# The last quarter of the first expert's output weights, narrowed in tiles 1 and 2 of the first expert instead of during attention

## The chip, the cores and the metric

The kernel runs on one core of a Trainium2 chip. The metric is the device time of one execution in microseconds (us). Engines are called as in the profile: PE (matmuls; PEld its weight loads), DVE, ACT, POOL and SP; each works through its own queue in the order in which the program issues to it. SP issues most of the DMAs here, POOL and ACT issue some.

## The reference

```python
# attention: 4 batches, 12 heads, 448 x 448 scores, head size 64
scores = einsum('bhij,hg->bgij', scale * q @ k.T, w_pre)      # heads mixed
attn   = einsum('bgij,gh->bhij', softmax(scores), w_post)     # mixed again
x      = (attn @ v)  as 1792 tokens x 768
# first expert (d_ff = 1024)
h = x @ w_in;  solu = h * softmax(h);  ln = layernorm(solu) * g_ln
x = ln @ w_out
# second expert (d_ff = 2048)
out = relu(x @ w_in2)**2 @ w_out2
```

## The kernel before

The four weight matrices of the experts arrive as 64-bit floats, which no engine computes with. The kernel turns them into 32-bit floats itself ("narrowing"): it takes pieces of 128 rows by 256 columns, loads the raw 64-bit words, squares the high word on ACT (to see which numbers are too small), makes a mask of that on POOL, puts the sign, exponent and mantissa together with three integer operations on DVE, and stores the 32-bit piece to a DRAM buffer (w1iD, w1oD, w2iD, w2oD), from which the matmul stages load it later. Every matrix is then split in two parts, a high part (a copy rounded by ACT) and a low part (the difference, on POOL), and each product takes three matmuls.

Four stages follow one another: attention (90 slots, to 382 us of the span), the first expert (14 tiles of 128 tokens, numbered m = 0 to 13), a short join, and the second expert (16 rounds).

**Narrowing in attention.** `w1pieces` (lines 413 and 414) lists 24 pieces of the first expert's input weights and 24 of its output weights (8 row blocks of 3 pieces). A planner in the slot loop gives the loads an even share of slots 5 to 70. For each piece POOL issues a load of 256 KB (`load_w1`, line 419), ACT squares, DVE does three operations of 256 columns, POOL two (`flush`, lines 102 and 103), ACT multiplies a piece of output weights by the layer norm's g (`scale_w1`, line 440), and SP stores 128 KB.

**Narrowing in the first expert.** `w2stream` (line 844) is a generator for the second expert's pieces. Its first step issues four loads on SP; the next two each issue a square on ACT and a mask on POOL; then every piece takes three steps, one DVE operation each (A, B, C: lines 887, 891, 893). Step A also issues the square and the mask of the piece after the next; step B the store of the piece before. `steps2(n)` takes n steps, and `rate(m, n)` says how many at each of four places of tile m: 0 up to tile 3 (`GT` is 3), n in tiles 4 to 12, n // 2 in tile 13.

**A tile of the first expert**, in the order of issue:

1. the load of tile m + 2's activations (SP, `load_x`);
2. `h1(m)`: 36 matmuls of 512 columns into one of two accumulators, which alternate;
3. `norm1(m)` up to its first pause: row maximum (DVE line 773), exponential (ACT 776), product with h (DVE 779), statistics (DVE 782, 784), root (POOL 786, 787);
4. place 1 for steps, then `nb` (DVE 790);
5. `zt(m - 1)`: eight transposes on PE (809), copied by ACT (811), low part by DVE (812);
6. in tiles 0 to 3 the rest of `norm1(m)` (ACT 794), then place 2 for steps;
7. `split_x(m + 2)`: high part by ACT (762), low part by POOL (763, 768 columns);
8. loads and splits of two row blocks of w_out, kk = 2m and 2m + 1 (SP 743, ACT 748, POOL 749), in tiles 0 to 3;
9. places 3 and 4 for steps, with an `out1` at each from tile 4 on: 24 matmuls that need the transposes of three tiles and all eight split blocks of w_out.

So the first `out1` comes in tile 4, and PE's own order in between is h1(2), transposes of tile 1, h1(3), transposes of tile 2, h1(4), transposes of tile 3, out1.

Of the kernel before, what the change touches and what calls it, by code (L numbers as in the profile page):

```python
# [11 lines left out]
AF = mybir.ActivationFunctionType  # L12
# [6 lines left out]
def kernel(  # L19
# [16 lines left out]
    nc = tc.nc  # L36
# [3 lines left out]
    NT, DM = out.shape  # L40
    F1 = w1_in.shape[1]
# [13 lines left out]
    scale = 1.0 / float(D) ** 0.5  # L55
# [7 lines left out]
    w1oD = dram.tile([F1, DM], F32, name="w1oD")  # L63
# [11 lines left out]
    g_sb = const.tile([128, F1 // 128], F32, name="g_sb")  # L75
# [64 lines left out]
    for b in range(B):  # L140
        for (i0, n) in CHUNKS:
# [10 lines left out]
            elif odd:  # L152
                k = nks[0] - 1
                order = [(1, k)] + order[:-2] + [(0, k)]
            for h, k in order:
                r = len(range(k, (n0, n - n0)[h], nks[h]))
# [9 lines left out]
    kk = {}  # L166
# [241 lines left out]
    WP = 256  # L408
# [2 lines left out]
    w1s = {}  # L411
    w1t = {}
    w1pieces = [(w1_in, w1iD, k, o) for k in range(CC) for o in range(0, F1, WP)]
    w1pieces += [(w1_out, w1oD, k, o) for k in range(F1 // 128) for o in range(0, DM, WP)]

    def load_w1(i):
        src, dst, k, o = w1pieces[i]
# [75 lines left out]
    def h1(m):  # L493
        t = xs.pop(m)
        pool = psi_p if m % 2 else psh_p
        ps = pool.tile([128, 2, 512], F32, tag="h", name="ps_h")
        for cc in range(CC):
            for (a, w) in ((0, 0), (0, 1), (1, 0)):
                for u in range(2):
                    nc.tensor.matmul(  # L500
                        out=ps[:, u],
                        lhsT=t[:, a, cc],
                        rhs=w1i[cc][:, w, u * 512:(u + 1) * 512],
                        start=(cc == 0 and a == 0 and w == 0),
                        stop=(cc == CC - 1 and a == 1),
                    )
            yield True
        hps[m] = ps

    def run(part):  # L510
        for _ in part:
            pass
# [215 lines left out]
    K1 = F1 // 128  # L728
# [12 lines left out]
    def load_w1_out(kk):  # L741
        r = wi1_p.tile([128, DM], F32, tag="wraw", name="w1oraw", bufs=3)
        nc.sync.dma_start(out=r, in_=w1oD[kk * 128:(kk + 1) * 128, :])
        return r

    def split_w1_out(kk, r):
        t = m1_p.tile([128, 2, DM], F32R, name=f"w1o{kk}")
        nc.scalar.copy(t[:, 0], r)
        nc.gpsimd.tensor_tensor(out=t[:, 1], in0=r, in1=t[:, 0].bitcast(F32), op=ALU.subtract)
        w1o.append(t)  # L750

    def load_x(m):
        r = wi1_p.tile([128, CC * 128], F32, tag="wraw", name="xraw", bufs=3)
        r = r.rearrange("p (c t) -> p c t", c=CC)
        nc.sync.dma_start(
            out=r, in_=xD[:, m * 128:(m + 1) * 128].rearrange("(c p) t -> p c t", p=128)
        )
        return r

    def split_x(m, r):  # L760
        t = m1b_p.tile([128, 2, CC, 128], F32R, tag="xs", name="xs", bufs=2)
        nc.scalar.copy(t[:, 0], r)
        nc.gpsimd.tensor_tensor(out=t[:, 1], in0=r, in1=t[:, 0].bitcast(F32), op=ALU.subtract)  # L763
        xs[m] = t
# [32 lines left out]
    GT = 3  # L797
# [37 lines left out]
    NE = F2 // FE  # L835
    KE = FE // 128
    FIRST = 60
    w2pieces = []
    for e in range(NE):
        w2pieces += [(w2_in, w2iD, c, e * FE) for c in range(CC)]  # L840
        w2pieces += [(w2_out, w2oD, e * KE + f, o) for f in range(KE) for o in range(0, DM, WP)]
    narrowed = []

    def w2stream(todo, nr, home):

        raws, ts, ready = {}, {}, []

        def load(i):
            if i in todo:
                src, dst, k, o = w2pieces[i]  # L850
                raws[i] = home(i, True)
                nc.sync.dma_start(out=raws[i], in_=src[k * 128:(k + 1) * 128, o:o + WP])

        def words(i):
            pair = raws[i].bitcast(U32).rearrange("p (n two) -> p n two", two=2)
            return pair[:, :, 0], pair[:, :, 1]

        def mask(i):

            if i in todo:  # L860
                t = ts[i] = home(i, False)
                nc.scalar.activation(out=t, in_=words(i)[1].bitcast(F32), func=AF.Square)  # L862
                nc.gpsimd.tensor_scalar(  # L863
                    out=t, in0=t, scalar1=2.0**-30, scalar2=2.0 - 2.0**-23, op0=ALU.is_ge, op1=ALU.mult
                )

        def store():
            i = ready.pop(0)
            src, dst, k, o = w2pieces[i]
            nc.sync.dma_start(out=dst[k * 128:(k + 1) * 128, o:o + WP], in_=ts.pop(i))  # L870
            narrowed.append(i)

        a = todo[0]
        for i in range(nr - 1):
            load(a + i)
        yield True
        mask(a)
        yield True
        mask(a + 1)
        yield True  # L880
        for i in todo:
            load(i + nr - 1)
            mask(i + 2)
            low, high = words(i)
            bits = ts[i].bitcast(U32)
            stt = nc.vector.scalar_tensor_tensor
            stt(out=bits, in0=high, scalar=3, in1=bits, op0=ALU.logical_shift_left, op1=ALU.bitwise_and)
            yield True
            if ready:
                store()  # L890
            stt(out=bits, in0=high, scalar=0xC0000000, in1=bits, op0=ALU.bitwise_and, op1=ALU.bitwise_or)
            yield True
            stt(out=bits, in0=low, scalar=29, in1=bits, op0=ALU.logical_shift_right, op1=ALU.bitwise_or)
            raws.pop(i)
            ready.append(i)
            yield True
        store()
        yield True
# [3 lines left out]
            return m1b_p.tile([128, WP], I64, tag="nraw", name="nraw", bufs=5)  # L902
        return m1b_p.tile([128, WP], F32, tag="nt", name="nt", bufs=5)

    stream = w2stream(range(FIRST), 5, home1)

    NTILE = NT // 128

    def rate(m, n):
        return 0 if m <= GT else n if m < NTILE - 1 else n // 2  # L910

    def steps2(n):
        for _ in range(n):
            next(stream, None)
# [4 lines left out]
    for m in range(NTILE):  # L919
        if m + 2 < NTILE:  # L920
            xr[m + 2] = load_x(m + 2)
        if m:
            run(h1(m))
        norm = norm1(m)
        next(norm)
        steps2(rate(m, 4))
        next(norm)
        if m > 0:
            zt(m - 1)
        if m <= GT:  # L930
            run(norm)
        steps2(rate(m, 6))
        if m + 2 < NTILE:
            split_x(m + 2, xr.pop(m + 2))
        for kk in range(len(w1o), min(K1, len(w1o) + 2)):
            wr[kk] = load_w1_out(kk)
        for kk in sorted(wr):
            split_w1_out(kk, wr.pop(kk))
        if m > GT and (m - 1) % GT == 0:
            outs += [((m - 1) // GT - 1, cc) for cc in range(CC)]  # L940
        for i in range(2):
            if outs:
                out1(*outs.pop(0))
            if i == 0:
                run(norm)
            steps2(rate(m, 4))


    outs += [((NTILE - 1) // GT, cc) for cc in range(CC)]
# [228 lines left out]
    def lows():  # L1178
        while low:
            r, f, t = low.pop(0)  # L1180
            hi, lo = [gt[:, a, f, t * HT:(t + 1) * HT] for a in range(2)]
            nc.vector.tensor_tensor(out=lo, in0=r, in1=hi.bitcast(F32), op=ALU.subtract)  # L1182
# [138 lines left out]
        t = wi2a_p.tile([128, HT], F32, tag=f"xb{i // 2 % 2}{i % 2}", name="nt", bufs=2)  # L1321
        return t[:, 0:WP]

    stream = w2stream(range(FIRST, len(w2pieces)), 4, home2)
    parts = []
    for q in range(NQ):
        p = q // NE
        work = plan(q)
        if q == NE - 1:
            parts = [((1, name), c) for name in ORDER for c in range(HC)]  # L1330
            load_xc(*parts[0][0])
            load_xc(*parts[HC][0])
        seq = SEQ_P if q < SW else SEQ
        for k, x in enumerate(seq):
            if isinstance(x, str):
                prod(q, x)
                after(q, x)
            elif q:
                y2(q - 1, x)
            lows()  # L1340
            for f, a in work.pop(k, []):
                f(*a)
            if parts:
                t, c = parts[0]
                if q == NE - 1 and (t[1] in ("p2", "p4") or t[1] in ("p7", "p3") and k < 7):
                    t = None
                if t:
                    parts.pop(0)
                    split_xc(*t, c)
                    i = ORDER.index(t[1]) + 2  # L1350
                    if c == HC - 1 and i < len(ORDER):
                        load_xc(1, ORDER[i])
            if q <= NE - 3:
                if q or k > 5:
                    steps2(2)
                if q == NE - 3 and k == len(seq) - 1:
                    run(stream)
                    next(mx)
            elif q == NE - 2 and k:
                next(mx, None)  # L1360
        assert not work
        if q < NE:
            assert len(narrowed) >= min(12 * (q + 2) + 6, len(w2pieces)), (q, len(narrowed))
    assert not parts
    for x in YO:
        y2(NQ - 1, x)
# [60 lines left out]
```

## Time and profile before

| what | value |
|---|---|
| median of three runs | 1085.63 us (1083.68 to 1088.42) |
| the profiled execution | 1085.38 us, of which its span (first to last instruction) 1083.6 us |
| PE busy | 1035.0 us, 96% of the span |
| DVE, ACT, POOL busy | 63%, 52%, 62% |
| mean granted clock of PE | 0.992 |

The span is the time from the first to the last instruction; 1.8 us of the execution lie outside it. Busy shares are averages over stages. What a change in one stage is worth has to be read in that stage, from the gaps of PE and from what ends them.

### The profile page before, as it was taken

How to read it: one execution, taken by the hardware profiler on the slowest of the kernel's cores; microseconds unless marked ns; L12 is line 12 of the kernel's file. 1: busy time of each engine (PE TensorE's matmuls, PEld its weight loads, DVE VectorE, ACT ScalarE, POOL GpSimd, SP SyncE). 2: the span in 40 equal slices, each digit the busy share in tenths (PEclk: the TensorE clock that was granted, in tenths of full speed). 3: DMA queues.
4: the chain of work that ended last, by engine and by line, in shares of the span. 5: the costliest groups of instructions: out<-in, count | busy, mean ns of one | idle time of the engine just before them, and what ended most of it. 6: DMA issues, size and time to landing. Idle time of an engine off the chain costs nothing.

```text
span 1083.6 us, 30106 instructions
## 1 busy us (share of the span) xinstructions
PE 1035.0 (96%) x12220; PEld 889.7 (82%) x12220; DVE 679.4 (63%) x1131; ACT 562.5 (52%) x1195; POOL 675.1 (62%) x868
## 2 busy tenths in 40 slices
PE   7798989989899899999999999999999999999998
PEld 3565656666666788999999989999999999999998
DVE  3576868767786346888876445787656833444444
ACT  4567667768777445444443446444334554444432
POOL 4567878878875737565645256666535757666620
PEclk9999999999999999999999999999999999999999
DMA  7678887878876624656555545444545521111102
GB/s 245 178 216 253 221 243 240 253 225 260 247 210 199 185 69 150 204 162 203 167 169 165 199 162 164 148 142 141 188 157 196 200 94 59 59 59 59 59 30 102
DMA packets 115914, 181.06 MB, mean 167 GB/s; under 512 B 24224, under 2 KB 87200, under 8 KB 115776
## 3 DMA queue, kind: packets, MB, share of 16 engines
q1 hardware_dynamic: 100276, 127.79, 38.5%
q0 software_dynamic: 12608, 48.55, 14.8%
q10 hardware_dynamic: 2892, 2.80, 0.9%
q8 instruction: 96, 1.57, 0.6%
q14 instruction: 42, 0.34, 0.1%
HBM read 102.42 MB, written 38.14 MB: 130 GB/s over the span
## 4 chain that ended last, share of the span: by engine, by line
PE 52%; POOL 3%; DVE 3%; issue 3%; DMA 2%; ACT 1%; SPq 0%; POOLq 0%; ACTq 0%
PE ps_y L1240 20%; PE ps_h L1169 17%; PE ps_o L823 8%; PE ps_h L500 7%; POOL ti L1097 1%; DMA w2oD<-nt 1%; DVE st L782 1%; DVE e L779 1%; POOL to L1105 1%; PE ps_tr L809 1%; DMA nraw<-in_moe_w_out_dram 0%; DMA ra<-w2iD 0%; ACT e L776 0%; POOL s L1077 0%; DVE nm L773 0%
## 5 line engine op out<-in xcount | busy, mean ns | idle before, releaser
L1240 PE MATMUL ps_y<-to,gt 128*128 128x384 f32 x1332 | 241.8, 336 | 2.5 <-POOL to L1105 1.8
L1240 PEld LDWEIGHTS ps_y<-to,gt 128*128 128x128 f32 x1332 | 233.6, 188 | 4.8 <-POOL to L1105 2.1
L1169 PE MATMUL ps_h<-xc,ti 128*128 128x448 f32 x1080 | 226.7, 364 | 0.6 <-ACT h L1185 0.6
L1169 PEld LDWEIGHTS ps_h<-xc,ti 128*128 128x128 f32 x1080 | 202.9, 189 | 13.5 <-ACT h L1185 1.0
L337 DVE COPY at<-ps_ring 128x840 f32<-128x840 f32 (+2 forms) x114 | 96.1, 854 | 75.4 <-PE ps_ring L307 75.1
L1251 DVE TENSOR_TENSOR y<-ps_y,y 128x768 f32<-128x768 f32 x97 | 92.4, 954 | 77.8 <-PE ps_y L1240 77.3
L863 POOL TENSOR_SCALAR nt<-nt 128x256 f32<-128x256 f32 x96 | 111.7, 1164 | 45.5 <-ACT nt L862 39.7
L307 PEld LDWEIGHTS ps_ring<-w,e 60*64 60x64 f32 x5040 | 94.2, 136 | 53.3 <-issue 32.1
L274 ACT ACTIVATE e<-ps_pre,nm 128x448 f32<-128x448 f32 x180 | 113.1, 638 | 30.6 <-DVE nm L267 27.3
L307 PE MATMUL ps_ring<-w,e 60*64 60x60 f32 x5040 | 101.6, 222 | 23.1 <-issue 18.1
L267 DVE TENSOR_REDUCE nm<-ps_pre 128x1 f32<-128x448 f32 x180 | 104.0, 616 | 27.9 <-PE ps_pre L256 26.4
L823 PE MATMUL ps_o<-zt,w1o 128*128 128x384 f32 (+1 forms) x720 | 120.6, 326 | 0.7 <-ACT o L831 0.5
L229 ACT COPY ssrc<-ps_ring 128x896 f32<-128x896 f32 x92 | 83.4, 907 | 68.2 <-PE ps_ring L222 68.0
L500 PE MATMUL ps_h<-w1i,xs 128*128 128x512 f32 x504 | 118.2, 391 | 0.7 <-POOL xs L763 0.6
L823 PEld LDWEIGHTS ps_o<-zt,w1o 128*128 128x128 f32 x720 | 116.9, 189 | 1.3 <-ACT o L831 0.8
L222 PE MATMUL ps_ring<-k,q 64*64 64x448 f32 x752 | 101.1, 558 | 11.3 <-issue 3.6
L1097 POOL TENSOR_TENSOR ti<-ra,ti 128x384 fp32r<-128x384 f32 x56 | 59.8, 1075 | 81.8 <-ACT ti L1096 80.9
L500 PEld LDWEIGHTS ps_h<-w1i,xs 128*128 128x128 f32 x504 | 93.9, 188 | 20.3 <-POOL xs L763 1.5
L1182 DVE TENSOR_TENSOR gt<-h,gt 128x448 fp32r<-128x448 f32 x64 | 50.3, 786 | 91.8 <-ACT gt L1187 87.1
L862 ACT ACTIVATE nt<-nraw 128x256 f32<-128x256 f32 x96 | 40.8, 433 | 121.4 <-DMA w2iD<-nt 36.8
L256 PE MATMUL ps_pre<-sdst,wpre_bd 64*64 64x448 f32 (+1 forms) x720 | 95.9, 552 | 5.0 <-DMA sdst<-ssrc 2.0
L1105 POOL TENSOR_TENSOR to<-ro,to 128x768 fp32r<-128x768 f32 x32 | 61.3, 1920 | 45.3 <-ACT to L1104 44.7
(111 smaller groups left out, 1523.0 us busy)
## 6 DMA issues: line engine op xcount, KB each, us to landing
sdst<-ssrc SPq DMA_DIRECT2D x166, 210.0 KB
nraw<-in_moe_w_in_dram SPq DMA_DIRECT2D x48, 256.0 KB
nraw<-in_moe_w_out_dram SPq DMA_DIRECT2D x48, 256.0 KB
ra<-w2iD POOLq DMA_DIRECT2D x32, 384.0 KB, 4.5
ro<-w2oD POOLq DMA_DIRECT2D x32, 384.0 KB, 3.7
w1raw<-in_moe_w_in_dram POOLq DMA_DIRECT2D x24, 256.0 KB, 6.9
w1raw<-in_moe_w_out_dram POOLq DMA_DIRECT2D x24, 256.0 KB, 5.6
w2iD<-nt SPq DMA_DIRECT2D x48, 128.0 KB
```

The costliest lines, as they stand in the source:

```text
L222: nc.tensor.matmul(out=ps[64 * u:64 * u + 64, e, 0:S], lhsT=qq[c][64 * e:64 * e + 64, p * n + u * half:p * n + u * half + 64], rhs=k[64 * ...
L256: nc.tensor.matmul(out=ps[b][64 * u:64 * u + 64, 0:S], lhsT=wpre_bd[64 * r:64 * r + m], rhs=ds[b][64 * r:64 * r + m], start=True, stop=True,)
L267: nc.vector.tensor_reduce(out=nm, in_=pres[s][b][:, 0:S], op=ALU.max, axis=AX.X, negate=True)
L274: nc.scalar.activation(out=e, in_=pres[s][b][:, 0:S], func=AF.Exp, bias=nms.pop((s, b)), scale=1.0, accum_out=sms[s][:, b:b + 1])
L307: nc.tensor.matmul(out=ps[64 * c:64 * c + 64, u, i0:i0 + PR], lhsT=ee[b][64 * u:64 * u + m, o:o + 64], rhs=w[64 * u:64 * u + m, b], start= ...
L337: nc.vector.tensor_copy(dst[:, :, :, RH * k:RH * k + RH], pv[h, :, n0:n1])
L500: nc.tensor.matmul(out=ps[:, u], lhsT=t[:, a, cc], rhs=w1i[cc][:, w, u * 512:(u + 1) * 512], start=(cc == 0 and a == 0 and w == 0), stop=( ...
L823: nc.tensor.matmul(out=ps[:, 0:width], lhsT=w1o[k][:, w, cc * 128:(cc + 1) * 128], rhs=zT[:, a, k, 0:width], start=(k == 0 and i == 0), st ...
L863: nc.gpsimd.tensor_scalar(out=t, in0=t, scalar1=2.0**-30, scalar2=2.0 - 2.0**-23, op0=ALU.is_ge, op1=ALU.mult)
L1169: nc.tensor.matmul(out=bank[b][:, 0:HT], lhsT=t[:, w, c], rhs=xc[xn][:, a, c], start=(first and j == 0 and c == 0 and i == 0), stop=(j == ...
L1240: nc.tensor.matmul(out=ps[:, u - u2[0], 0:DM // 2], lhsT=gt[:, a, f, o:o + 128], rhs=w[:, v, f, u * (DM // 2):(u + 1) * (DM // 2)], start= ...
L1251: nc.vector.tensor_tensor(out=yo, in0=po, in1=yo, op=ALU.add)
```

## The change

The last two of the eight row blocks of w_out (six of 48 pieces) leave attention's list and become the first six pieces of the stream that runs in the first expert. Their loads begin at the end of tile 0, their steps run in tiles 1 and 2 at half the rate (2, 3, 2 and 2 steps at the four places), and the rest of them is taken in one go ahead of h1(3), after which the stream for the second expert begins as before, in tile 4. In tiles 0 to 3 place 2 moves behind `split_x`. As the pieces are now stored without the factor g, the two blocks are multiplied by it when they are loaded whole (768 columns, ACT) ahead of their split. The last numbers of pieces are shifted by six.

```diff
     w1pieces = [(w1_in, w1iD, k, o) for k in range(CC) for o in range(0, F1, WP)]
-    w1pieces += [(w1_out, w1oD, k, o) for k in range(F1 // 128) for o in range(0, DM, WP)]
+    KL = F1 // 128 - 2
+    w1pieces += [(w1_out, w1oD, k, o) for k in range(KL) for o in range(0, DM, WP)]
...
     def split_w1_out(kk, r):
         t = m1_p.tile([128, 2, DM], F32R, name=f"w1o{kk}")
+        if kk >= KL:
+            nc.scalar.activation(out=r, in_=r, func=AF.Copy, scale=g_sb[:, kk:kk + 1])
         nc.scalar.copy(t[:, 0], r)
...
-    w2pieces = []
+    w2pieces = [(w1_out, w1oD, k, o) for k in range(KL, K1) for o in range(0, DM, WP)]
+    NL = len(w2pieces)
...
-    stream = w2stream(range(FIRST), 5, home1)
+    stream = w2stream(range(NL), 5, home1)
...
     def rate(m, n):
-        return 0 if m <= GT else n if m < NTILE - 1 else n // 2
+        return 0 if m in (0, GT) else n if GT < m < NTILE - 1 else n // 2
...
             xr[m + 2] = load_x(m + 2)
+        if m == GT:
+            run(stream)
+            stream = w2stream(range(NL, NL + FIRST), 5, home1)
         if m:
             run(h1(m))
...
-        steps2(rate(m, 6))
+        if m > GT:
+            steps2(rate(m, 6))
         if m + 2 < NTILE:
             split_x(m + 2, xr.pop(m + 2))
+        if m <= GT:
+            steps2(rate(m, 6))
         for kk in range(len(w1o), min(K1, len(w1o) + 2)):
...
             steps2(rate(m, 4))
+        if m == 0:
+            next(stream)
...
-    stream = w2stream(range(FIRST, len(w2pieces)), 4, home2)
+    stream = w2stream(range(NL + FIRST, len(w2pieces)), 4, home2)
```

## Rows read from the trace of the kernel before

**Rows 1.** The page, busy time of each engine over the span
```profile
PE 1035.0 (96%) x12220; PEld 889.7 (82%) x12220; DVE 679.4 (63%) x1131; ACT 562.5 (52%) x1195; POOL 675.1 (62%) x868
```
**Rows 2.** Busy time by stretch: attention's, then the first expert's tiles 4 on
```profile
core 0: us, PE busy (x) PEld busy (x) DVE busy (x) ACT busy (x) POOL busy (x), PEclk, DMA share, GB/s
40.00:60.00 20.00, 14.50 (x354) 10.58 (x349) 8.77 (x13) 9.85 (x24) 9.38 (x19) 0.91 0.82 215
...
40.00:280.00 240.00, 211.69 (x5414) 146.60 (x5409) 169.37 (x309) 162.31 (x398) 190.22 (x338) 0.98 0.81 236
280.00:340.00 60.00, 58.26 (x1595) 40.24 (x1591) 46.15 (x86) 46.42 (x115) 41.84 (x77) 1.00 0.73 221
...
427.30:561.80 134.50, 134.50 (x707) 122.77 (x708) 112.56 (x216) 56.65 (x111) 81.97 (x73) 1.00 0.63 184
```
**Rows 3.** What PE waited for, 40 to 280 us: total us, times, longest
```profile
PE ps_ring L307 <- issue: 18.1, 12, 3.4
PE ps_ring L222 <- issue: 3.6, 2, 2.5
PE ps_pre L256 <- issue: 1.5, 2, 1.3
```
**Rows 4.** Timeline, DVE in tiles 2 and 3: start, duration, instruction, [idle before]
```profile
403.79 1.23 DVE L773 TENSOR_REDUCE nm<-ps_h 128x1 f32<-128x1024 f32 x1 [1.32 <-PE ps_h L500]
...
410.58 1.28 DVE L812 TENSOR_TENSOR zt<-ps_tr,zt 128x512 fp32r<-128x512 f32 x2
412.84 1.23 DVE L773 TENSOR_REDUCE nm<-ps_h 128x1 f32<-128x1024 f32 x1 [0.98 <-PE ps_h L500]
```
**Rows 5.** Timeline, POOL's split of the activations in tiles 1 and 2
```profile
403.24 1.84 POOL L763 TENSOR_TENSOR xs<-xraw,xs 128x768 fp32r<-128x768 f32 x1 [2.27 <-ACT xs L762]
...
412.74 1.85 POOL L763 TENSOR_TENSOR xs<-xraw,xs 128x768 fp32r<-128x768 f32 x1 [2.27 <-ACT xs L762]
```
**Rows 6.** Timeline, from tile 3's last norm step to the first out1
```profile
419.75 1.25 ACT L794 ACTIVATE e<-e,nb,rs 128x1024 f32<-128x1024 f32 x1 [3.42 <-DVE nb L790]
...
422.03 1.04 PE L809 MATMUL ps_tr<-id_sb,e 128*128 128x128 f32 x8
...
423.59 3.64 POOL L749 TENSOR_TENSOR w1o<-w1oraw,w1o 128x768 fp32r<-128x768 f32 x2
...
427.29 3.91 PE L823 MATMUL ps_o<-zt,w1o 128*128 128x384 f32 x21 [0.20 <-POOL w1o L749]
```
**Rows 7.** Groups of instructions: busy us, mean ns of one, idle before
```profile
L863 POOL TENSOR_SCALAR nt<-nt 128x256 f32<-128x256 f32 x96 | 111.7, 1164 | 45.5 <-ACT nt L862 39.7
...
L440 ACT ACTIVATE w1t<-w1t,g_sb 128x256 f32<-128x256 f32 x24 | 10.9, 510 | 0.0
...
L748 ACT CAST w1o<-w1oraw 128x768 fp32r<-128x768 f32 x8 | 6.3, 829 | 0.0
```
**Rows 8.** Timeline, steps A, B, C on DVE alone, and beside POOL's subtractions
```profile
432.52 0.42 DVE L891 SCALAR_TENSOR_TENSOR nt<-nraw,nt 128x256 uint32<-128x256 uint32 x1
...
433.84 0.43 DVE L891 SCALAR_TENSOR_TENSOR nt<-nraw,nt 128x256 uint32<-128x256 uint32 x1
...
435.27 2.02 POOL L763 TENSOR_TENSOR xs<-xraw,xs 128x768 fp32r<-128x768 f32 x1
435.63 1.95 DVE L893 SCALAR_TENSOR_TENSOR nt<-nraw,nt 128x256 uint32<-128x256 uint32 x1
...
647.43 2.38 POOL L1097 TENSOR_TENSOR ti<-ra,ti 128x384 fp32r<-128x384 f32 x2
647.83 1.11 DVE L891 SCALAR_TENSOR_TENSOR nt<-nraw,nt 128x256 uint32<-128x256 uint32 x1
648.98 1.12 DVE L893 SCALAR_TENSOR_TENSOR nt<-nraw,nt 128x256 uint32<-128x256 uint32 x1
```
**Rows 9.** Timeline, steps on DVE beside three masks on POOL
```profile
447.29 3.82 POOL L863 TENSOR_SCALAR nt<-nt 128x256 f32<-128x256 f32 x3
...
449.76 0.42 DVE L887 SCALAR_TENSOR_TENSOR nt<-nraw,nt 128x256 uint32<-128x256 uint32 x1
```

More of the change, by code (lines that the diff above doesn't have):

```diff
@@ L1362 @@
         if q < NE:
-            assert len(narrowed) >= min(12 * (q + 2) + 6, len(w2pieces)), (q, len(narrowed))
+            assert len(narrowed) >= min(NL + 12 * (q + 2) + 6, len(w2pieces)), (q, len(narrowed))
     assert not parts
```

## The prediction, made before the changed kernel ran

> **What bounds the kernel now.** I read the page's busy table first: PE is busy 96% of the span [rows 1], so the change can matter only where PE has gaps or where it opens new ones. The table by stretch shows where the gaps are. From tile 4 of the first expert on PE is busy 134.50 of 134.50 us [rows 2]: a delay that PE meets ahead of tile 4 is never made up, it moves the end. In attention, 40 to 280 us, PE is busy 211.69 of 240 us, and its waits there are mainly of the kind "issue", 23.2 us in all, for which the profile names no work [rows 2, 3]. They lie in the stretch in which the pieces are loaded, with a DMA share of 0.81; from 280 to 340 us, at 0.73, there is none of them and PE is busy 58.26 of 60 us.
>
> The timeline of tiles 1 to 3 of the first expert decides this change. No out1 runs there yet, so a tile lasts only as long as h1 and eight transposes: tile 2's row maximum starts at 403.79, tile 3's at 412.84, 9.05 us [rows 4]. In that time DVE goes through one chain (maximum, exponential on ACT, product, statistics, root on POOL, nb, zt) that ends at 410.58 + 1.28 = 411.86. So DVE has 1.32 us free ahead of tile 2's maximum and 0.98 us ahead of tile 3's, and both starts wait for PE: PE leads by one us a tile. At the far end ACT finishes tile 3's normalisation at 419.75 + 1.25 = 421.00, and PE transposes it from 422.03: 1.03 us of slack [rows 6].
>
> **What it removes from attention.** Six pieces: six POOL loads, twelve POOL and eighteen DVE operations, six squares and six scalings, and 6 x 384 KB = 2.36 MB of DMA. All those engines run beside a PE that is busy or waits for "issue", so their time is worth nothing directly. What can be gained is part of the 23.2 us. The stretch moves 236 GB/s x 240 us = 56.6 MB, so it loses 4.2% of its traffic. In proportion that is 1 us. On a straight line from 23.2 us at a share of 0.81 to none at 0.73, a share lower by 0.034 is worth 9.9 us. The line rests on two points, and I take 3 us, nearer to the proportion; for the range 0 to 10. The list's share of slots stays 5 to 70, so nothing that follows the last piece starts earlier.
>
> **What it adds to tiles 1 to 3, without contention.** Counting the generator's steps through the places: tile 1 gets all its masks but one (0 to 4) and the DVE operations A0 to A2 (seven); tile 2 gets the last mask and B2 to A5 (nine); B5 and C5 come ahead of tile 3's maximum. A step on DVE alone costs 0.42 to 0.50, three of them 433.84 - 432.52 = 1.32 us [rows 8]: 18 cost 7.9 us, and every one stands in DVE's queue ahead of a row maximum. I follow the queue.
>
> Tile 1: the normalisation is untouched, as place 1 holds only masks. POOL ends the split of xs(3) at 403.24 + 1.84 = 405.08 [rows 5]. The mask of piece 2 stands behind it, 1.16 [rows 7], and A2 waits for that mask: 405.08 + 1.16 + 0.42 = 406.7. Tile 2's maximum stands behind A2, so it starts at 406.7 instead of 403.79: +2.9.
>
> Tile 2 runs the same, 2.9 later (B2 and C2 fill the gap in which DVE waits for POOL's root). xs(4) ends on POOL at 412.74 + 1.85 [rows 5] + 2.9 = 417.5, mask 5 at 418.65, A5 at 419.1, then B5 and C5, 0.85: tile 3's maximum starts at 419.95 instead of 412.84: +7.1.
>
> Tile 3: ACT's last norm step ends at 421.00 + 7.1 = 428.1; PE's h1(4) is done by then and PE stands idle. The transposes start at 428.1 instead of 422.03: PE is 6.1 late. Then come the blocks 6 and 7 of w_out: on ACT, behind xs(5), two scalings and two casts. A cast of 768 columns is 0.83, a scaling of 256 is 0.51 [rows 7]; a scaling of 768 lies between 0.51 and 1.53, and I take the cast's 0.83. ACT, with the cast of xs(5) of the same shape ahead of them, ends at 428.1 + 5 x 0.83 = 432.25, and POOL's last low part, 1.82 each [rows 6], at 434.4. Before, that low part ended at 423.59 + 3.64 = 427.23 and PE went on at 427.29. So PE is 7.1 us late at the first out1. The loads of these blocks wait for the last store, which waits for C5 (420.0); ACT turns to them only at 428.9, 9 us later, so I cost that wait at nothing. This lower end is +7.1.
>
> **With contention.** A step on DVE that meets a subtraction on POOL does not run beside it: 1.95 us instead of 0.43 beside a subtraction of 768 columns, and beside two of 384 columns in a row one step is held by each, 1.11 and 1.12, the engines taking turns [rows 8]. In tiles 1 and 2 POOL has three such subtractions per tile, xs and two of w_out. The one of xs costs nothing more, since A2 (A5) waits for the mask behind it anyway. Those of w_out follow the mask, just where C1 and A2 (A5 and B5) stand in DVE's queue: each holds one step for 1.85 and lets one of 0.42 through, 2.3 us, so four cost 9.2 and the upper end is +16.3. I take three of the four, +14.0: in tile 1 the two blocks' data is there early, in tile 2 their loads stand on SP behind a store that waits for C2, and may come too late to be in the way.
>
> Here a rule of the Trainium skill says more than the row. While three masks run on POOL (3.82 us), steps on DVE take 0.42 [rows 9]: masks do not hold steps. "SBUF — State Buffer", section "Who interferes with whom", says that a DVE instruction with two inputs in SBUF contends with any GpSimd instruction that reads SBUF, which a mask does; the trace disagrees with that for masks and agrees for subtractions.
>
> **The rest.** The first four loads are issued at the end of tile 0, a tile of 9 us ahead of the first square; hidden, and if they were late, the square would hold up ACT's next work, the copies of tile 0's transposes. Moving place 2 behind `split_x` puts xs ahead of a mask on POOL and costs nothing. The first stream in tile 4 starts from the same place as before. The shift of piece numbers by six turns the order of two buffers in the second expert: nothing. PE's idle time can lower its clock: a stretch of 20 us with 5.5 us of gaps shows 0.91 [rows 2], 1.8 us of full-speed work; the two new gaps of 6 us and more can bring up to that once on the path. Range only.
>
> **The sum.** 1085.4 (the profiled execution; the median is 0.25 above) + 14.0 - 3 = 1096.4.
>
> **Rivals.** (1) The subtractions seldom meet the steps: +7.1 - 3, 1089.5. For it: a shift of half a us decides who is first. Against: the two engines took turns wherever they met. (2) The other side: attention gains the straight line's 10 us and more, because gaps of "issue" also bring the clock down [rows 2], while the first expert loses only the lower end or less, because PE's lead of one us a tile and late data for w_out swallow it: 1085.4 - 10 + 5 = 1080. It decides from the point where attention's waits fall by over 5.4 us more than PE's loss in tiles 1 to 3. Against: 18 steps in some 3 us of free DVE time. (3) Masks hold steps as well: six by 1.16, of which A2 and A5 wait for two anyway, so 4.6 us are new: 1101. This is the rule of the page named above, against the row. (4) The work fits in after all, and attention gains 3: 1082.5, no change that can be measured.
>
> **How the numbers follow.** Forecast 0.55, rival 1 0.20, rival 2 0.09, rival 3 0.06, rival 4 0.10. A measurement tells 0.5%, 5.4 us, from no change, that is 1080.2 to 1091.1 about the median. Slower: the forecast, rival 3 and part of rival 1 (0.10): 0.71. Same: rest of rival 1, rival 4: 0.20. Faster: 0.09. The range reaches from rival 1 with a larger gain in attention (1085.4 + 7.1 - 6.5 = 1086) to the upper end of the first expert with one fall of the clock and little gain (1085.4 + 16.3 + 1.8 - 0 = 1103.5); it leaves out rivals 2 and 4, about 0.2.
>
> **What would show it.** In the changed profile: tile 2's row maximum 3 to 8 us behind the end of h1(2), tile 3's 7 to 17 behind that of h1(3), each right behind a step A or C of the stream; steps of 1.9 us beside POOL's subtractions at line 749; PE idle for 6 us and more ahead of the transposes of tiles 2 and 3; attention ending a few us earlier than 382.2, with less "issue". Wrong it would be if DVE's row maxima still followed PE's h1 at once, or if attention's end moved by more than 10 us.

## The result: slower by 1.2%, and the profile after

In the comparison that followed the prediction the changed kernel took 1102.7 us at the median of six runs, the kernel before 1086.0; the ratio is 1.0131, with a 95% interval of 1.0093 to 1.0168. Two more comparisons of the same two kernels (below) gave 1.0113 (1.0064 to 1.0163) and 1.0124 (1.0084 to 1.0165). Together that is 13 us. The forecast was 1096.4 us, 11 us more than the profiled execution of before, in a range of 1086.0 to 1103.5.

The profiled execution of the changed kernel took 1109.3 us, the longest of its six, so I do not read the difference of the two spans (23.9 us) as the change's; I read the stages. PE's busy time beside that of [rows 1]:

```profile
PE 1044.8 (94%) x12220; PEld 892.9 (81%) x12220; DVE 688.8 (62%) x1131; ACT 563.0 (51%) x1191; POOL 668.2 (60%) x856
```

The same 12220 matmuls are busy for 9.8 us longer, since PE ran a part of them at the lower of its two clock levels (a granted clock of 0.50). How much of that lies on the path is read below. Next, what PE waited for between 380 and 700 us (total us, times, longest):

```profile
PE ps_tr L812 <- ACT e L797: 10.8, 3, 6.2
PE ps_y L1252 <- POOL to L1117: 1.8, 1, 1.8
PE ps_h L501 <- POOL xs L766: 0.6, 1, 0.6
PE ps_o L826 <- ACT o L834: 0.4, 1, 0.4
```

The new wait is that of the transposes for ACT's last step of the normalisation. The split blocks of w_out (line 752) do not stand in the list. That alone does not clear the scalings and the later loads of blocks 6 and 7, because out1 runs partly at the lower clock here and may come to the last block just as it is ready; two of the experiments decide it. Now the first expert by itself, from the end of attention (382.21 before, 391.42 after) to the start of h1(5). Columns are those of [rows 2]; first the kernel before, then the changed one:

```profile
382.21:431.73 49.52, 48.49 (x240) 40.77 (x237) 27.03 (x48) 25.41 (x41) 28.09 (x25) 1.00 0.41 120
```
```profile
391.42:455.51 64.09, 52.65 (x241) 44.34 (x237) 42.95 (x64) 30.03 (x50) 34.52 (x30) 0.92 0.42 129
```

The stretch lasts 14.6 us longer. PE is idle for 11.4 us of it (1.0 before), and busy for 4.2 us more with the same matmuls, at a mean clock of 0.92. From h1(5) to the end both kernels take the same: 1083.6 - 431.73 = 651.9 and 1107.5 - 455.51 = 652.0. What the first expert loses ahead of tile 5 is not made up. The remaining 9.2 us lie in attention of this one execution; a later profile of the same kernel has attention's end at 382.24, where it was before.

The timeline of DVE and POOL shows tile 1, in the changed kernel (A, B, C are lines 891, 895 and 897 there, the mask 867, the splits 766 and 752, the row maximum 776):

```profile
411.51 0.58 DVE L891 SCALAR_TENSOR_TENSOR nt<-nraw,nt 128x256 uint32<-128x256 uint32 x1
412.13 0.42 DVE L895 SCALAR_TENSOR_TENSOR nt<-nraw,nt 128x256 uint32<-128x256 uint32 x1
412.58 1.85 POOL L766 TENSOR_TENSOR xs<-xraw,xs 128x768 fp32r<-128x768 f32 x1
412.59 2.12 DVE L897 SCALAR_TENSOR_TENSOR nt<-nraw,nt 128x256 uint32<-128x256 uint32 x1
...
414.51 1.13 POOL L867 TENSOR_SCALAR nt<-nt 128x256 f32<-128x256 f32 x1
414.63 0.61 DVE L891 SCALAR_TENSOR_TENSOR nt<-nraw,nt 128x256 uint32<-128x256 uint32 x1
...
415.28 0.42 DVE L895 SCALAR_TENSOR_TENSOR nt<-nraw,nt 128x256 uint32<-128x256 uint32 x1
...
415.72 3.83 POOL L752 TENSOR_TENSOR w1o<-w1oraw,w1o 128x768 fp32r<-128x768 f32 x2
415.74 2.11 DVE L897 SCALAR_TENSOR_TENSOR nt<-nraw,nt 128x256 uint32<-128x256 uint32 x1
417.77 2.07 DVE L891 SCALAR_TENSOR_TENSOR nt<-nraw,nt 128x256 uint32<-128x256 uint32 x1
...
419.76 1.22 DVE L776 TENSOR_REDUCE nm<-ps_h 128x1 f32<-128x1024 f32 x1
```

Three of the seven steps take over 2 us, each begun within 0.3 us of a subtraction of 768 columns on POOL. Then the row maximum of tile 2 starts at 419.76, though h1(2) ended at 412.96: 6.8 us late. In [rows 4] it followed PE at once. Tile 2 ends the same way, with both subtractions of w_out holding the last two steps:

```profile
432.32 4.05 POOL L752 TENSOR_TENSOR w1o<-w1oraw,w1o 128x768 fp32r<-128x768 f32 x2
...
432.74 1.94 DVE L895 SCALAR_TENSOR_TENSOR nt<-nraw,nt 128x256 uint32<-128x256 uint32 x1
434.70 1.95 DVE L897 SCALAR_TENSOR_TENSOR nt<-nraw,nt 128x256 uint32<-128x256 uint32 x1
436.58 1.21 DVE L776 TENSOR_REDUCE nm<-ps_h 128x1 f32<-128x1024 f32 x1
...
444.78 1.97 PE L812 MATMUL ps_tr<-id_sb,e 128*128 128x128 f32 x8 [4.46 <-ACT e L797]
```

Tile 3's maximum is 14.5 us behind h1(3), which ended at 422.04, and the transposes of tile 3 come 53.36 us after attention's end instead of 39.82 [rows 6]: 13.5 us late. They take 1.97 us instead of 1.04, at a granted clock of 0.50, after PE had waited 4.46 us. From there on the delay stays what it is: tile 3's row maximum starts 45.16 us after attention's end instead of 30.63, 14.5 us late, and h1(5) is 14.6 us late.

### The profile page after: what moved, and what is told of

It is laid out like the page before. It is cut to its first block, busy times and chain, and to the rows that moved or that the text cites. A ratio compares the mean times of both kernels' runs of the same rounds, so it can differ in the third digit from the quotient of the medians.

```text
span 1107.5 us, 30089 instructions
## 1 busy us (share of the span) xinstructions
PE 1044.8 (94%) x12220; PEld 892.9 (81%) x12220; DVE 688.8 (62%) x1131; ACT 563.0 (51%) x1191; POOL 668.2 (60%) x856
## 4 chain that ended last, share of the span: by engine, by line
PE 51%; DVE 4%; issue 3%; POOL 3%; DMA 2%; ACT 1%; SPq 0%; POOLq 0%; ACTq 0%
PE ps_y L1252 19%; PE ps_h L1181 17%; PE ps_o L826 8%; PE ps_h L501 6%; POOL ti L1109 1%; PE ps_tr L812 1%; DVE st L785 1%; DVE e L782 1%; DVE nt L891 1%; DMA w2oD<-nt 1%; POOL to L1117 1%; DVE nt L895 1%; ACT e L779 0%; DVE nm L776 0%; DMA ra<-w2iD 0%
## 5 line engine op out<-in xcount | busy, mean ns | idle before, releaser
L1181 PEld LDWEIGHTS ps_h<-xc,ti 128*128 128x128 f32 x1080 | 202.9, 189 | 13.5 <-ACT h L1197 1.0
L867 POOL TENSOR_SCALAR nt<-nt 128x256 f32<-128x256 f32 x102 | 119.6, 1172 | 42.9 <-ACT nt L866 36.4
L222 PE MATMUL ps_ring<-k,q 64*64 64x448 f32 x752 | 104.1, 573 | 12.5 <-DMA q<-in_qT_dram 3.5
L866 ACT ACTIVATE nt<-nraw 128x256 f32<-128x256 f32 x102 | 43.5, 433 | 112.7 <-DMA w2iD<-nt 37.0
```

The costliest lines, as they stand in the source:

```text
L222: nc.tensor.matmul(out=ps[64 * u:64 * u + 64, e, 0:S], lhsT=qq[c][64 * e:64 * e + 64, p * n + u * half:p * n + u * half + 64], rhs=k[64 * ...
L867: nc.gpsimd.tensor_scalar(out=t, in0=t, scalar1=2.0**-30, scalar2=2.0 - 2.0**-23, op0=ALU.is_ge, op1=ALU.mult)
L1181: nc.tensor.matmul(out=bank[b][:, 0:HT], lhsT=t[:, w, c], rhs=xc[xn][:, a, c], start=(first and j == 0 and c == 0 and i == 0), stop=(j == ...
```

## The experiments

All times are against the kernel before on the same chip, as ratios with 95% intervals. "First expert" means the stretch above: 49.5 us before, 64.1 after.

**The two halves apart.** First only the removal:

```diff
-    w1pieces += [(w1_out, w1oD, k, o) for k in range(F1 // 128) ...]
+    KL = F1 // 128 - 2
+    w1pieces += [(w1_out, w1oD, k, o) for k in range(KL) ...]
...
-        nc.sync.dma_start(out=r, in_=w1oD[kk * 128:(kk + 1) * 128, :])
+        ks = kk if kk < KL else kk - 2
+        nc.sync.dma_start(out=r, in_=w1oD[ks * 128:(ks + 1) * 128, :])
```

> Only the removal from attention: the six pieces are not narrowed at all, and the split of blocks 6 and 7 of w_out loads blocks 4 and 5 a second time (that part of the computation is left out). The first expert has no added steps. Theory of the prediction: attention is 3 us shorter, so about 1083 us against 1086 of the kernel before, with the waits of the kind issue between 40 and 280 us down from 23 to about 20 us. Rival (the waits follow the DMA share on a straight line): 10 us shorter, 1076. Second rival (attention's gaps are a matter of chance from run to run and do not follow six pieces of 48): no difference, 1086, and attention's end scattered by several us between profiles.

Measured: 0.9940 (0.9908 to 0.9973), about 6.5 us faster, between the theory's 3 and the straight line's 10. Attention ended at 376.7 in its profile, the first expert took 49.5 us as before:

```profile
376.71:426.23 49.52, 48.49 (x241) 40.77 (x237) 27.16 (x48) 25.59 (x41) 28.12 (x25) 1.00 0.41 120
```

Waits of the kind "issue" came to 19.4 us between 40 and 280 us, near the 20 expected, but they scatter too much to be a sign: 16.9 in the second run of this kernel, 16.2 and 22.5 in the two runs of one kernel further below. Six pieces of 48 weigh more in attention than their share of the traffic.

Then only the steps (changed kernel, all 48 pieces narrowed in attention, the six narrowed again into a spare buffer):

```diff
-    w1pieces += [(w1_out, w1oD, k, o) for k in range(KL) ...]
+    w1pieces += [(w1_out, w1oD, k, o) for k in range(F1 // 128) ...]
...
-        if kk >= KL:
-            nc.scalar.activation(out=r, in_=r, func=AF.Copy, scale=...)
...
-    w2pieces = [(w1_out, w1oD, k, o) for k in range(KL, K1) ...]
+    w2pieces = [(w1_out, spD, k, o) for k in range(KL, K1) ...]
```

> Only the steps: attention narrows all 48 pieces as before, and tiles 1 and 2 narrow the same six pieces once more into a spare buffer that nobody loads; blocks 6 and 7 come from attention, with no scaling and no wait for the stream. Theory (the steps and their contention are the cost, the scalings and the later loads of blocks 6 and 7 are hidden): the first expert takes 63 to 64 us from the end of attention to the start of h1(5), attention is as before, about 1100 us. Rival (the late blocks 6 and 7 with their scalings are what PE waits for): 55 us and about 1091.

Measured: 1.0158 (1.0110 to 1.0205), and this stretch of the first expert:

```profile
383.12:447.79 64.67, 52.24 (x241) 44.26 (x237) 44.30 (x67) 27.89 (x48) 36.70 (x31) 0.89 0.41 128
```

64.7 us without any scaling and without a block that waits for the stream: the steps are the whole loss, and the rival with the late blocks falls. Tile 3's row maximum comes 45.16 us after attention's end, as in the changed kernel. The two halves add up to 17 - 6.5 = 10.5 us, against 13 us for the change; the intervals allow that.

**What the subtractions cost.** The changed kernel with POOL's subtraction of blocks 2 to 5 of w_out put out of the way:

```diff
-        nc.gpsimd.tensor_tensor(out=t[:, 1], in0=r, in1=t[:, 0]..., op=ALU.subtract)
+        if 2 <= kk < 6:
+            nc.gpsimd.memset(t[:, 1].bitcast(F32), 0.0)
+        else:
+            nc.gpsimd.tensor_tensor(out=t[:, 1], in0=r, in1=t[:, 0]..., op=ALU.subtract)
```

> The changed kernel with POOL's subtraction of blocks 2 to 5 of w_out (the ones issued in tiles 1 and 2) put in place by a memset of the same tile, which reads nothing (the low parts of these blocks are left out of the computation). Theory with contention: in the changed kernel's profile three or four steps on DVE of about 2 us stand beside these subtractions; without them the row maximum of tile 2 starts some 4 us earlier and that of tile 3 some 8 us earlier, and the first expert from the end of attention to the start of h1(5) shrinks from 64.1 us to about 56 to 57.5 (49.5 before the change): 7 us faster than the changed kernel. Rival (only the place of the steps in DVE's queue counts): the two maxima stay where they are, 64 us, no difference from the changed kernel.

Measured: 1.0021 (0.9982 to 1.0060), 11 us below the changed kernel (7 were expected; the intervals are 4 to 5 us to either side). First the stretch of the first expert, then the same place of tile 1 as above (here the steps are lines 894, 898 and 900, the memset 753, the row maximum 779), then that of tile 3 and what PE waited for at out1:

```profile
384.02:441.71 57.69, 49.12 (x241) 40.47 (x238) 36.54 (x64) 28.98 (x48) 29.36 (x30) 1.00 0.47 144
```
```profile
407.22 0.61 DVE L894 SCALAR_TENSOR_TENSOR nt<-nraw,nt 128x256 uint32<-128x256 uint32 x1
407.87 0.42 DVE L898 SCALAR_TENSOR_TENSOR nt<-nraw,nt 128x256 uint32<-128x256 uint32 x1
408.29 1.42 POOL L753 MEMSET w1o<- 128x768 f32 x2
408.33 0.43 DVE L900 SCALAR_TENSOR_TENSOR nt<-nraw,nt 128x256 uint32<-128x256 uint32 x1
408.67 0.42 DVE L894 SCALAR_TENSOR_TENSOR nt<-nraw,nt 128x256 uint32<-128x256 uint32 x1
409.01 1.22 DVE L779 TENSOR_REDUCE nm<-ps_h 128x1 f32<-128x1024 f32 x1
...
422.80 1.22 DVE L779 TENSOR_REDUCE nm<-ps_h 128x1 f32<-128x1024 f32 x1
```
```profile
PE ps_o L829 <- POOL w1o L755: 1.0, 1, 1.0
```

The last two steps take 0.43 and 0.42 us beside the memset, which writes and does not read; beside the subtractions they took 2.11 and 2.07. The first expert falls from 64.1 to 57.7 us, just above the 56 to 57.5 expected, and counted from attention's end the row maxima come earlier by 3.4 us (tile 2) and 6.4 us (tile 3), where 4 and 8 were expected. The 6.4 us of the second are the whole gain of the stretch, so the clock, which stays at 1.00 here, has no part in it. The memsets are also shorter than the subtractions, but the masks that POOL did next were done long before the steps that read them. What remains, 8.2 us at tile 3's row maximum, is the steps' place in the queue, which the prediction had at 7.1. Two steps are still held in it (2.11 and 2.05 us), beside POOL's split of the activations.

The wait at out1 shows what the lower clock hid in the changed kernel: at full clock PE comes to the last block of w_out 1.0 us before it is ready. The scalings are not the reason. From the end of ACT's last norm step of tile 3 to the end of POOL's last low part it is 6.25 us here (430.96 to 437.21) and 6.24 in the changed kernel, both with the scalings, and 6.23 before, without them [rows 6]. This chain is late by what tile 3's row maximum is late; at the transposes 1.0 us of that fell into the 1.03 us that PE had in hand there, at the block it did not.

**The order of the splits.** Place 2 back ahead of the split of the activations:

```diff
-        if m > GT:
-            steps2(rate(m, 6))
+        steps2(rate(m, 6))
         if m + 2 < NTILE:
             split_x(m + 2, xr.pop(m + 2))
-        if m <= GT:
-            steps2(rate(m, 6))
```

> The changed kernel with place 2 back ahead of the split of the activations in tiles 1 and 2. Theory of the prediction (the order of mask and split costs or gives little, since A2 and A5 wait for the mask behind the split only if nothing else holds them): within 2 us of the changed kernel, as the blocks by the subtractions of w_out remain. Rival (splitting the activations first is what keeps h1 fed): h1(4) and h1(5) wait for the low part by one mask and one square more, and the kernel is 1.5 to 3 us slower than the changed one.

Measured: 1.0070 (1.0040 to 1.0100); the first expert took 62.2 us (from 380.87 to 443.10). That is 1.9 us shorter than in the first profile of the changed kernel and 3.1 shorter than in the second (below), and by the ratios the kernel is some 5 us faster than the changed one, with intervals that overlap. "Within 2 us" is just met by one of these figures and missed by the others; the rival, which had it slower, falls. Splitting the activations first costs time, and the end of tile 1 shows where:

```profile
403.16 2.00 POOL L766 TENSOR_TENSOR xs<-xraw,xs 128x768 fp32r<-128x768 f32 x1
403.52 1.93 DVE L897 SCALAR_TENSOR_TENSOR nt<-nraw,nt 128x256 uint32<-128x256 uint32 x1
...
405.37 2.07 DVE L891 SCALAR_TENSOR_TENSOR nt<-nraw,nt 128x256 uint32<-128x256 uint32 x1
407.36 1.21 DVE L776 TENSOR_REDUCE nm<-ps_h 128x1 f32<-128x1024 f32 x1
```

With the third mask ahead of the split A2 no longer waits for it, and A1 and B1 ran before the subtraction began; two steps of tile 1 are held instead of three, and the row maximum comes 1.9 us earlier. The rest of the difference in ratio lies outside this stretch and is not explained.

**Which part of the removal counts.** The kernel before, with the six pieces loaded and stored but not worked on:

```diff
     def narrow_w1(i):
         src, dst, k, o = w1pieces[i]
+        if dst is w1oD and k >= KL:
+            for step in range(4):
+                if step == 3:
+                    w1f[i] = None, w1raw.pop(i)
+                yield True
+            return
...
```

> The kernel before with the six pieces loaded and stored at their old places in attention, but without the engines' work on them (no square, no mask, no steps, no scaling; the stored words are raw halves, that part is left out). Theory: attention's gain without the six pieces comes from less DMA traffic, so with the transfers kept there is none: 1.000 of the time before, waits of the kind issue about 23 us. Rival: it comes from the engines' work (ACT's squares that wait for a load, POOL's time ahead of the weights), so the gain stays: 0.994 to 0.996.

Measured: 1.0003 (0.9967 to 1.0039): no gain, as the theory of the traffic says. But the interval touches that of the removal, and the "issue" waits do not decide either (20.7 us here between 40 and 372 us, 19.4 with the removal). This kernel also keeps POOL's issuing of the six loads, which it does not tell from the traffic. That attention pays for the transfers is likely, not shown.

**The changed kernel again.**

> The changed kernel as it is, once more beside the kernel before, since attention's length scatters from run to run. From the parts: the steps alone cost 15 us in the first expert (profiles), the removal alone gave 6.5 us (3 to 10) in attention. If the parts add up: 1.008 of the time before (+8 us). If attention gains nothing here (as the first comparison, 1.0131, and its profile suggested): 1.013 again.

Measured: 1.0113 (1.0064 to 1.0163), between the two; of this comparison only the times are used.

> The changed kernel a third time, for a second profile of it: the first expert from the end of attention to the start of h1(5) was 64.1 us in the first profile (49.5 before), while attention's end was 9.2 us later, though it has six pieces less. Theory (the first expert's part is fixed by the queues, attention's length scatters): 64 to 65 us again, attention's end anywhere from 376 to 392 us, the ratio 1.008 to 1.014. Rival (attention is really longer in the changed kernel): attention ends at 388 us or later again.

Measured: 1.0124 (1.0084 to 1.0165). Attention ended at 382.24, so it is not longer in the changed kernel, and the first expert took 65.3 us:

```profile
382.24:447.53 65.29, 53.56 (x241) 45.39 (x237) 44.17 (x67) 30.35 (x51) 35.62 (x30) 0.90 0.42 127
```

The steps in it match those of the first profile one by one (tile 2's maximum 410.55, tile 3's 427.38, the transposes of tile 3 53.34 us after attention's end). Only the clock differs, and with it the first out1s.

**Steps where DVE waits anyway.** If places and meetings are the cost, other places should remove it. The next two kernels call each operation of the stream by hand: A and B behind the statistics, while POOL takes the root; masks behind that root; what is left behind the transposes' low part; the scaling by pieces on ACT, so that a whole block needs none. First one row block (three pieces, the other three stay in attention), then both:

```diff
-    stream = w2stream(range(NL), 5, home1)
+    SCHED = {(0, "L"): "L0 L1 L2 L3 L4", (0, 1): "m0", (0, 2): "A0 B0 m1 m2", (0, 3): "C0",
+             (1, 0): "S0 W0 L5", (1, 2): "A1 B1 C1 A2 B2 m3 m4", (1, 3): "C2 A3",
+             (2, 0): "S1 S2 W1 W2", (2, 2): "B3 C3 A4 B4 C4 m5", (2, 3): "A5 B5 C5",
+             (2, 4): "S3 S4 W3 W4", (3, 0): "S5 W5"}
...
```

This is the second kernel's list. L is a load, m a square and a mask, A, B and C are the steps, S a scaling, W a store. The keys are the tile and the place: L ahead of tile 0's norm, 0 behind the exponential, 1 behind the statistics, 2 behind the root, 3 ahead of the split of the activations, 4 at the tile's end.

> Only the last row block (three pieces) moved, its nine steps placed by hand where DVE waits anyway: A and B behind the statistics, while POOL takes the root; C and the next A behind the transposes' low part; the mask of the first piece ahead of tile 0's root, the two others behind it; the scaling by piece on ACT, ahead of the store. Theory (the cost of the change is the place of its steps and their meeting with POOL's subtractions, not their number): the first expert takes 49.5 to 50.5 us from the end of attention to the start of h1(5), PE waits at no transposes; attention gains half of what six pieces gain; 0.997 of the time before (-3 us). Rival (any step in tiles 0 to 2 delays the row maxima by its length and more): 53 to 55 us and 1.000 to 1.002.

Measured: 0.9998 (0.9966 to 1.0030); the first expert took 50.0 us (385.39 to 435.39). The nine steps cost 0.5 us there, as expected; the gain that half of the pieces should have brought in attention (3 us) did not show.

> Both row blocks moved, with the same placing: 18 steps in tiles 0 to 2, five in a row behind the statistics of tiles 1 and 2, which meet no subtraction on POOL. Theory: what does not fit in the gaps costs its 0.44 us each and no more; the first expert takes 51 to 53 us instead of the changed kernel's 64, attention gains 6.5: 0.995 to 0.998 of the time before, 10 us and more below the changed kernel. Rival: 57 to 58 us, as without the subtractions of w_out, and 1.002.

Measured: 0.9967 (0.9937 to 0.9997); the first expert took 52.1 us:

```profile
380.23:432.28 52.05, 48.82 (x241) 40.64 (x237) 33.07 (x65) 28.86 (x50) 34.89 (x30) 1.00 0.53 159
```

All 18 steps are in it. Here are those of tile 1, five beside POOL's root and two masks and the last two with the row maximum behind them (steps are lines 938, 940 and 942 here, masks 931):

```profile
398.19 0.38 DVE L938 SCALAR_TENSOR_TENSOR nt<-nraw,nt 128x256 uint32<-128x256 uint32 x1
...
398.61 0.42 DVE L940 SCALAR_TENSOR_TENSOR nt<-nraw,nt 128x256 uint32<-128x256 uint32 x1
398.70 0.76 POOL L790 TENSOR_TENSOR rs<-rs,eps_sb 128x1 f32<-128x1 f32 x1
399.07 0.42 DVE L942 SCALAR_TENSOR_TENSOR nt<-nraw,nt 128x256 uint32<-128x256 uint32 x1
399.41 0.42 DVE L938 SCALAR_TENSOR_TENSOR nt<-nraw,nt 128x256 uint32<-128x256 uint32 x1
399.55 2.37 POOL L931 TENSOR_SCALAR nt<-nt 128x256 f32<-128x256 f32 x2
399.86 0.50 DVE L940 SCALAR_TENSOR_TENSOR nt<-nraw,nt 128x256 uint32<-128x256 uint32 x1
...
401.55 0.41 DVE L942 SCALAR_TENSOR_TENSOR nt<-nraw,nt 128x256 uint32<-128x256 uint32 x1
401.89 0.41 DVE L938 SCALAR_TENSOR_TENSOR nt<-nraw,nt 128x256 uint32<-128x256 uint32 x1
...
402.22 1.21 DVE L774 TENSOR_REDUCE nm<-ps_h 128x1 f32<-128x1024 f32 x1
```

No step there exceeds 0.50 us, masks on POOL or not, and none of the 18 exceeds 0.65. Once more:

> The kernel with two blocks placed by hand once more: its ratio 0.9967 had an interval that reached to 0.9997. Theory (2.5 us lost in the first expert, 4 to 6.5 won in attention): 0.996 to 0.999. Rival (attention's gain in the first comparison was chance): 1.000 to 1.003.

Measured: 0.9993 (0.9957 to 1.0030). The first run's gain is not confirmed: the kernel is about as fast as the one before, and 1.2 to 1.6% faster than the changed one.

To take the last 2.5 us, PE's waits for POOL's split were attacked too, with h1 of tiles 2 to 4 taking all matmuls with the high part first (the list of matmuls sorted by that part):

> Both row blocks moved and placed by hand as in the kernel with two blocks placed, and in h1 of tiles 2 to 4 all matmuls with the high part of the activations ahead of all with the low part, so that PE does not reach the low part before POOL has it. Theory: the waits for POOL's split of the activations (2.1 us in three places) go, the first expert takes 50 us instead of 52, about 0.995 of the time before. Rival (DVE's chain sets these tiles, and PE only waits at another place): 52 us, 0.997.

Measured: 0.9983 (0.9953 to 1.0012), the first expert 51.9 us (380.45 to 432.39). The rival holds: the waits for the split are gone, but 2.2 us of waits at the transposes stand in their place. DVE's chain sets these tiles.

**The removal again.**

> Only the removal from attention once more (the six pieces are not narrowed, blocks 6 and 7 load 4 and 5 again; that part is left out). The first comparison gave 0.994, 3 to 10 us. The changed kernel's sum (13 us slower, 15 us of them in the first expert) leaves about 2 us for attention, the kernel with two blocks placed 6. If six: 0.994 again; if two: 0.997 to 0.999. In both the profile's first expert is 49.5 us.

Measured: 0.9935 (0.9901 to 0.9969), so about 7 us, twice; the first expert took 49.6 us (377.51 to 427.10). Both intervals overlap that of the kernel with the transfers kept (from 0.9967) by very little.

## Why the prediction was right

**The bound.** That PE cannot make up a loss ahead of tile 5 held to about 1 us: from h1(5) to the end it is 651.9 us before, and 652.0 and 650.8 in the two profiles of the changed kernel.

**The path.** It was the one predicted: the steps stand in DVE's queue ahead of a row maximum, and tile 3's row maximum is late by as much as h1(5) is (14.5 and 14.6 us in the changed kernel, 8.2 and 8.2 without the subtractions). Of the signs named ahead one came only in part and one not at all: PE's idle time was 6.2 us ahead of tile 2's transposes but 4.5 ahead of tile 3's, since h1(4) took 10.47 us there instead of 8.76, and attention did not end earlier in either profile (391.42 and 382.24).

**The queue without contention.** Predicted 2.9 and 7.1 us at the two row maxima; measured 3.4 and 8.2, with the subtractions of w_out out of the way. A part of the difference can be read in tile 1: the split of the activations, of which the prediction said that it costs nothing more, holds C0 there, so that C1 still stands ahead of A2 when the mask is done, and A2 starts 0.44 us after the mask. Nor did it cost nothing to move place 2 behind that split: the stretch is 1.9 us shorter, or more, without the move.

**Contention.** Predicted: four meetings possible, three taken, 2.3 us each. All four came (C1, A2, B5 and C5, at 1.94 to 2.11 us), so the loads of w_out's blocks were not late enough to be out of the way, as I had feared for tile 2. But each cost 1.6 us (6.4 us for four, between the kernels with and without the subtractions), not 2.3. The prediction took the whole subtraction and a step of 0.42 that it lets through, but the steps' own time stood in the lower end already; the row that it read [rows 8] has a held step 1.95 - 0.43 = 1.5 us longer, no more. So its three meetings came to 6.9 us and the four that happened cost 6.4. Two errors cancelled, and that the sum is so near (14.0 us predicted, 14.6 and 15.8 in the two profiles) is luck to that extent.

**Scalings and late blocks.** Measured on ACT a scaling takes 0.93 us (the prediction took 0.83), and it adds nothing to the path. The prediction let POOL's last low part wait for five operations on ACT and had it at 434.4, where its own terms give 432.25 + 1.82 = 434.07. POOL's three subtractions behind the first cast, 428.1 + 0.83 + 1.84 + 3.64 = 434.41, are longer than ACT's chain, so the 7.1 us at the first out1 hold without the scalings: they are what ACT is late.

**The clock.** Left out of the sum, up to 1.8 us in the range. The lower clock lengthened matmuls in both profiles of the changed kernel, but on the path it cost next to nothing in the first (h1(5) is 14.6 us late, tile 3's row maximum 14.5), where out1's slower start fell into the time in which it would have waited for the last block (from the end of the last low part to h1(5) it is 4.55 us there and 4.50 at full clock without the subtractions), and 1.3 us in the second (15.8 and 14.5).

**Attention.** Predicted 3 us of gain, between 0 and 10. Measured alone: 6.5 and 7, so this term was too small. In the sum of the changed kernel it seems less: 13 us slower in all, where the first expert's profiles show 14.6 and 15.8 us, leaves 1 to 3. The same difference of stretch and ratio leaves 5 to 6 us in the kernel without the subtractions and in that with place 2 back, and 3 to 6 in the kernels with two blocks placed by hand, which all have the same six pieces out. Whether six pieces gain less in the changed kernel, or the intervals (4 us each) hide it, stays open.

**Masks.** The rival in which masks hold steps too falls: 0.41 to 0.50 us beside two masks in the last fence, and 0.66 at most beside masks in the whole traces of before and after, where in tiles 1 and 2 a held step takes around 2. Of the Trainium skill's rule ("SBUF — State Buffer", section "Who interferes with whom") the trace bears out the contention of steps with subtractions and its absence with a memset, which only writes, but not a contention with masks.

**The other rivals.** That subtractions seldom meet the steps: all four did. That the work fits in: in the places that the change gave it, it did not; in others 18 steps cost 2.5 us. That attention's gain outweighs the loss: it would have taken twice what was measured.

## What to carry to other kernels

Before moving work into a stage, write out the in-order queue of the engine that takes it: what counts is what stands behind each new instruction there, not how busy the engine is. DVE's busy time in this stretch was 27 of 49.5 us, and eight us of new work cost 15. Look next at which of the other engine's instructions the new ones will meet, since the same 18 steps cost 15 us in one set of places and 2.5 in another.

## What the runs showed of the hardware

A DVE operation with two inputs in SBUF and a POOL subtraction of two inputs in SBUF took turns (1.93 to 2.12 us instead of 0.42 in tiles 1 and 2), whichever tile they worked on; beside a POOL memset the same operation took 0.42 to 0.43, beside a mask 0.41 to 0.66. PE's granted clock fell to its lower level after waits of 6.2 and 4.5 to 4.8 us (0.92 and 0.90 in the mean of the changed kernel's stretch), which made transposes take 1.97 instead of 1.04 us. With waits of 2.9 and 3.1 us it stayed at 1.00 in the kernel without the subtractions, but with waits of 3.1 and 3.4 us it fell in the kernel with place 2 back (0.92 in the mean of that stretch), so the length of a wait does not tell by itself. And attention's length scatters: its end lay between 376.7 and 391.4 us over thirteen profiles of kernels with 42 to 48 pieces in it, and the changed kernel alone had 382.2 and 391.4, so the span of a single profile says little about a change of 10 us here.
